# An earlier layernorm pipeline around the inverse FFT rounds, and a first MLP matmul loop in quarters instead of halves

## The chip, the cores and the metric

The kernel runs on one core of one Trainium2 chip. The metric is the device time of one execution, in microseconds. "Span" is the length of the one profiled execution; timed runs are longer by some 1.8 us. In the profile PE is TensorE, DVE is VectorE, ACT is ScalarE, POOL is GpSimd and SPq is the queue of SyncE, which here issues the DMA transfers. L512 is line 512 of the kernel file.

## The reference

A long convolution by FFT sits between two layernorms and is followed by two MLPs. Sequence length is 2048 and width 640, so there are 16 tiles of 128 positions. Cut to what matters:

```python
h = _layernorm(x) * (1 + ca) + sa
x = x + ga * conv_h3(h, A_k, A_v, ...)       # kv -> FFT -> product -> inverse FFT -> q * y
h = _layernorm(x) * (1 + cb) + sb            # "first" layernorm below, with its affine
# inside the MLP block, on h:
h1 = gelu(_layernorm(h) @ w1)                # "second" layernorm; w1 is 640 x 640
hs = shift_by_1_1_2_2(h1) @ w2               # four column groups shifted along the sequence
x1 = h + hs
out = x + gb * (x1 + gelu(_layernorm(x1) @ w3) @ w4)   # third layernorm; w3 is 640 x 1728
```

## The kernel before

The change lies in the stretch from the last inverse FFT step to the end of the first MLP loop. The inverse FFT delivers the 16 tiles in six rounds of three tiles (the last has one). For each tile VectorE forms y*q and adds the residual, ScalarE squares it, POOL turns the sums into mean and inverse deviation, VectorE does the affine of the first layernorm, ScalarE squares again, POOL finishes again, VectorE normalises into `hn`, and a DMA transpose writes it into `hnT`, on which the first MLP matmul works.

```python
def ln_finish(li, t0, t1):                    # eight tiny POOL instructions, 1 to 3 columns each
    n = t1 - t0
    bq, var, tmp = ...                        # [P, 4] F32
    nc.gpsimd.tensor_scalar(bq, s1, 1.0 / D, None, ALU.mult)
    nc.gpsimd.tensor_tensor(var, bq, bq, ALU.mult)
    nc.gpsimd.tensor_scalar(var, var, -1.0, EPS, ALU.mult, ALU.add)
    nc.gpsimd.tensor_scalar(tmp, s2, 1.0 / D, None, ALU.mult)
    nc.gpsimd.tensor_tensor(var, var, tmp, ALU.add)
    nc.gpsimd.tensor_tensor(rstds[:, li, t0:t1], var, mhalf, ALU.pow)
    nc.gpsimd.tensor_tensor(tmp, bq, rstds[:, li, t0:t1], ALU.mult)
    nc.gpsimd.tensor_scalar(nbs[:, li, t0:t1], tmp, -1.0, None, ALU.mult)

def consume(A, yps2):                         # y*q, residual, square
    t = work.tile([P, 4, 160], BF, name="yq", tag="yq")
    for h in range(2):
        nc.vector.tensor_tensor(t[:, 2*h:2*h+2, :], yps2[h], qv[:, 2*h:2*h+2, :], ALU.mult)
    nc.vector.scalar_tensor_tensor(x1_all[:, A, :], t, 1.0, x1_all[:, A, :], ..., accum_out=sums[:, 0, 0, A:A+1])
    nc.scalar.activation(junk, x1_all[:, A, :], ACT.Square, accum_out=sums[:, 0, 1, A:A+1])

def ln_stage_b(tiles):                        # affine of the first layernorm, square
    for t in tiles:
        nc.vector.tensor_scalar(u, x1_all[:, t, :], rstds[:, 0, t:t+1], nbs[:, 0, t:t+1], ALU.mult, ALU.add)
        nc.vector.tensor_tensor(u, u, cb1, ALU.mult)
        nc.vector.scalar_tensor_tensor(h_all[:, t, :], u, 1.0, sbv, ..., accum_out=sums[:, 1, 0, t:t+1])
        nc.scalar.activation(junk, h_all[:, t, :], ACT.Square, accum_out=sums[:, 1, 1, t:t+1])

def ln_stage_d(tiles):                        # normalise, transpose
    for t in tiles:
        hn = work.tile([P, D], BF, name="hn", tag="hn")           # two buffers
        nc.vector.tensor_scalar(hn, h_all[:, t, :], rstds[:, 1, t:t+1], nbs[:, 1, t:t+1], ALU.mult, ALU.add)
        nc.sync.dma_start_transpose(hnT[:, :, t*P:(t+1)*P], hn)

def pipeline_step(r):                         # called after round r
    if 0 <= r - 1 < NR: ln_finish(0, ...)     # of round r-1
    if 0 <= r - 2 < NR: ln_stage_b(rounds[r - 2])
    if 0 <= r - 3 < NR: ln_finish(1, ...)     # of round r-3
    if 0 <= r - 4 < NR: ln_stage_d(rounds[r - 4])

w3_sb, w4_sb = ...                            # in memory that the FFT and q have used; loads issued here

for hf in range(2):                           # first MLP loop: two halves of 1024 positions
    for fb in range(ND):                      # five blocks of 128 output columns
        ps2 = psB.tile([P, 2, 512], F32, name="ps_l1", tag="q2")
        for scl in range(2):
            for b in range(ND): nc.tensor.matmul(ps2[:, scl, :], w1 block, hnT[:, b, 512 positions])
        # GELU of the 1024 positions, shifted, cut where a column group or a partition rule asks for it
        for (p0, p1) in _legal_pieces(...):
            nc.scalar.activation(gsT[p0:p1, fb, ...], psf[p0:p1, ...], ACT.Gelu_apprx_tanh)
# ... second MLP loop (tile by tile: matmul, residual, square, ln_finish(2), normalise, transpose),
# ... third and fourth MLP loops, output
```

The order in which instructions stand in each engine's queue is chosen when the kernel is built, by a scheduler that works from the order of the source; what it chose can be read in the trace.

## Time and profile before

The kernel took 496.61 us, the median of 4 runs (495.66 to 497.45). The profiled execution has a span of 493.8 us.

| us from the span's start | before |
|---|---|
| first y*q on VectorE | 248.7 |
| first normalise (`hn`) | 285.7 |
| last square of the two layernorms ends on ScalarE | 301.9 |
| first GELU starts | 305.6 |
| last transpose lands | 317.6 |
| last GELU ends | 328.7 |
| second MLP loop starts on VectorE | 327.6 |
| third MLP loop starts on TensorE | 347.7 |

The first lines of the profile's page give the busy time of each engine; the next line gives the chain that ended last. No engine is busy for more than two thirds of the span: the kernel is a relay of stages, and each stage has to be read by itself.

```profile
span 493.8 us, 8042 instructions
...
PE 314.8 (64%) x3092; PEld 183.4 (37%) x3092; DVE 234.0 (47%) x565; ACT 224.2 (45%) x319; POOL 91.4 (19%) x227
...
PE 38%; DVE 23%; DMA 17%; ACT 10%; issue 5%; SPq 4%; POOL 2%; DVEq 0%; POOLq 0%; ACTq 0%
```

The chain of waits, in order of time, for the end of the stage (start, duration, what). A piece "DMA KSb<-hn" is a transpose, from its issue to its landing.

```profile
302.61 2.57 DMA KSb<-hn
305.27 0.46 DVE hn L519
...
314.57 0.46 DVE hn L519
315.05 2.58 DMA KSb<-hn
...
317.76 1.25 PE ps_l L568 x5
319.04 1.00 ACT B L579
```

The chain steps from a transpose (about 2.6 us) to the normalise that waited for its buffer (0.46 us) and on to the next transpose. There are two `hn` buffers, so the tiles come in pairs. The last transpose lands at 317.63, and the second half of the GELUs can only then begin.

ScalarE's own timeline (start, duration, line, instruction, output and input; in brackets how long it was idle before, and what ended that):

```profile
301.11 0.74 ACT L514 ACTIVATE junk<-KSb 128x640 bf16<-128x640 bf16 x1 [1.08 <-DVE B L558]
...
301.96 1.28 ACT L579 ACT_TABLE_LOAD   x1
305.59 3.09 ACT L579 ACTIVATE B<-ps_l 128x1024 bf16<-128x1024 f32 x3 [2.35 <-PE ps_l L568]
...
315.06 0.28 ACT L588 ACTIVATE B<-ps_l 128x31 bf16<-128x31 f32 x2
319.04 1.00 ACT L579 ACTIVATE B<-ps_l 128x992 bf16<-128x992 f32 x1 [3.69 <-PE ps_l L568]
...
326.61 2.06 ACT L579 ACTIVATE B<-ps_l 32x1024 bf16<-32x1024 f32 x2
```

In this trace ScalarE works through its queue in order. The last square of the layernorms (301.11) is followed by every GELU of the loop. The first GELU waited 2.35 us for TensorE: in this kernel a group of matmuls covers 1024 positions, so it needs eight transposed tiles. The tenth normalise started at 303.83 after a wait that ended on a transpose; with two buffers that is the eighth tile's, which therefore landed at about 303.8, just before the five last matmuls of that group. From 315.34 ScalarE idles 3.69 us, for the last eight tiles.

The queue of SyncE (start, time over which the issues are spread, what, count):

```profile
277.42 0.39 SPq L553 DMA_DIRECT2D B<-in_B_w_dram  x1
278.05 0.70 SPq L552 DMA_DIRECT2D B<-in_B_w_dram  x1
286.12 2.77 SPq L520 DMA_TRANSPOSE KSb<-hn  x2
...
293.24 23.01 SPq L520 DMA_TRANSPOSE KSb<-hn  x14
```

Two weight loads of 2080 and 2160 KB (w4 and w3) were issued just before the first transposes.

### The profile page before, as it was taken

How to read it: one execution, taken by the hardware profiler on the slowest of the kernel's cores; microseconds unless marked ns; L12 is line 12 of the kernel's file. 1: busy time of each engine (PE TensorE's matmuls, PEld its weight loads, DVE VectorE, ACT ScalarE, POOL GpSimd, SP SyncE). 2: the span in 40 equal slices, each digit the busy share in tenths (PEclk: the TensorE clock that was granted, in tenths of full speed). 3: DMA queues.
4: the chain of work that ended last, by engine and by line, in shares of the span. 5: the costliest groups of instructions: out<-in, count | busy, mean ns of one | idle time of the engine just before them, and what ended most of it. 6: DMA issues, size and time to landing. Idle time of an engine off the chain costs nothing.

```text
span 493.8 us, 8042 instructions
## 1 busy us (share of the span) xinstructions
PE 314.8 (64%) x3092; PEld 183.4 (37%) x3092; DVE 234.0 (47%) x565; ACT 224.2 (45%) x319; POOL 91.4 (19%) x227
## 2 busy tenths in 40 slices
PE   0115859759778200683043109799399999999994
PEld 0112433549557200673011003245134444445552
DVE  3049518204699765791089995137200000344443
ACT  2165552787667422383035445677945444000000
POOL 1045100000002222000038787024600000000000
PEclk9999998989999855698555557999879999999998
DMA  8991694340205532007900485303440000011111
GB/s 278 399 232 33 106 118 56 56 182 33 56 9 148 159 87 79 16 3 147 279 3 3 140 267 100 66 2 66 93 55 0 1 0 1 20 38 40 39 41 41
DMA packets 74463, 43.14 MB, mean 87 GB/s; under 512 B 56952, under 2 KB 72632, under 8 KB 74168
## 3 DMA queue, kind: packets, MB, share of 16 engines
q1 hardware_dynamic: 71592, 38.69, 32.6%
q10 hardware_dynamic: 2064, 2.62, 1.6%
q0 software_dynamic: 768, 1.31, 1.2%
q8 instruction: 24, 0.39, 0.3%
q14 instruction: 15, 0.12, 0.1%
HBM read 29.50 MB, written 7.86 MB: 76 GB/s over the span
## 4 chain that ended last, share of the span: by engine, by line
PE 38%; DVE 23%; DMA 17%; ACT 10%; issue 5%; SPq 4%; POOL 2%; DVEq 0%; POOLq 0%; ACTq 0%
PE ps_l L640 14%; PE ps_l L631 12%; DMA B<-in_A_v_dram 5%; DMA B<-q_scr 4%; PE ps_s L169 4%; ACT B L261 4%; DMA KSb<-hn 4%; DVE B L263 3%; DVE B L502 2%; DVE yq L493 2%; PE ps_l L599 2%; DVE KSb L512 2%; DMA xt<-in_A_q_dram 2%; DVE TA L183 2%; SPq L342 2%
## 5 line engine op out<-in xcount | busy, mean ns | idle before, releaser
L631 PE MATMUL ps_l<-KSb,B 128*128 128x512 bf16 (+1 forms) x280 | 63.9, 391 | 8.4 <-DMA KSb<-xn 8.4
L643 DVE TENSOR_TENSOR bo<-ps_l,KSb 128x512 bf16<-128x512 f32 x16 | 11.1, 691 | 109.4 <-PE ps_l L640 109.4
L261 ACT CAST B<-ps_s 128x1024 bf16<-128x1024 f32 (+1 forms) x46 | 38.9, 961 | 18.3 <-PE ps_s L157 13.3
L631 PEld LDWEIGHTS <-B 128*128 128x128 bf16 (+1 forms) x280 | 28.0, 101 | 43.9 <-issue 7.2
L192 PE MATMUL ps_s1i<-ESs,TA 64*128 64x128 bf16 x320 | 20.5, 230 | 37.0 <-DVE TA L183 37.0
L169 PE MATMUL ps_s<-B,Gs 64*64 64x320 bf16 x512 | 38.5, 305 | 7.0 <-DVE B L263 3.9
L209 PE MATMUL ps_out<-B,Hs 32*32 32x160 bf16 x512 | 13.5, 310 | 40.2 <-DVE yq L493 39.0
L169 PEld LDWEIGHTS <-Gs 64*64 64x64 bf16 x512 | 35.0, 110 | 10.5 <-issue 6.8
L568 PE MATMUL ps_l<-KSb,Gs 128*128 128x512 bf16 x100 | 25.0, 413 | 20.8 <-DMA KSb<-hn 19.9
L361 PE MATMUL ps_ksh<-kT,diagw 128*128 128x512 bf16 x80 | 21.8, 432 | 19.8 <-DVE diagw L326 16.2
L505 ACT ACTIVATE junk<-B 128x640 bf16<-128x640 bf16 x16 | 11.8, 737 | 37.4 <-DVE B L502 37.4
L438 POOL TENSOR_SCALAR ln_rstd<-ln_mv 128x1 f32<-128x1 f32 x16 | 4.1, 256 | 130.5 <-DVE ln_mv L435 130.5
L157 PE MATMUL ps_s<-F1bd,B 128*128 128x256 bf16 x160 | 21.5, 272 | 9.1 <-ACT B L261 5.5
L640 PE MATMUL ps_l<-B,B 128*128 128x512 bf16 (+1 forms) x160 | 27.3, 301 | 0.0
L192 PEld LDWEIGHTS <-TA 64*128 64x128 bf16 x320 | 13.5, 102 | 37.2 <-issue 37.2
L442 ACT ACTIVATE xh<-xt,ln_nb,ln_rstd 128x640 bf16<-128x640 bf16 x16 | 14.7, 920 | 26.8 <-DVE ln_nb L440 15.6
L493 DVE TENSOR_TENSOR yq<-ps_out,B 128x320 bf16<-128x320 f32 x32 | 14.2, 480 | 24.5 <-DMA B<-q_scr 24.5
L263 DVE CAST B<-ps_s 128x640 bf16<-128x640 f32 (+1 forms) x26 | 24.4, 965 | 0.0
L261 ACT CAST B<-ps_s1i 128x1024 bf16<-128x1024 f32 x20 | 19.3, 1017 | 10.8 <-PE ps_s1i L192 10.8
L568 PEld LDWEIGHTS <-Gs 128*128 128x128 bf16 x100 | 10.3, 105 | 35.4 <-DMA KSb<-hn 17.7
L209 PEld LDWEIGHTS <-Hs 32*32 32x32 bf16 x512 | 5.5, 100 | 48.0 <-issue 47.9
L640 PE MATMUL ps_l<-B,Gs 128*128 128x512 bf16 (+1 forms) x128 | 22.6, 299 | 0.0
(119 smaller groups left out, 648.5 us busy)
## 6 DMA issues: line engine op xcount, KB each, us to landing
KSb<-in_w_mod_dram SPq DMA_DIRECT2D x1, 4800.0 KB
B<-in_A_v_dram ACTq DMA_DIRECT2D x1, 2560.0 KB
B<-in_A_k_dram SPq DMA_DIRECT2D x1, 2560.0 KB
xt<-in_A_q_dram SPq DMA_DIRECT2D x64, 40.0 KB
B<-kv_scr SPq DMA_DIRECT2D x1, 2560.0 KB
q_scr<-qt SPq DMA_DIRECT2D x16, 160.0 KB
B<-in_A_q_dram SPq DMA_DIRECT2D x4, 640.0 KB
B<-q_scr SPq DMA_DIRECT2D x1, 2560.0 KB
```

The source lines that it names most:

```text
L157: nc.tensor.matmul(psv[:, ml, :], lhsT=xf[:, m * 128:(m + 1) * 128], rhs=rhs, start=True, stop=True)
L169: nc.tensor.matmul(ps[64 * g:64 * g + 64, kl, 0:320], lhsT=Gs[64 * g:64 * g + 64, k2, c, cp, :], rhs=T1[64 * g:64 * g + 64, c * 32 + k2, : ...
L192: nc.tensor.matmul(psv[:, g, ql, :], lhsT=T[64 * g:64 * g + 64, cp, 4 * lq:4 * lq + 4, :].rearrange("p a k -> p (a k)"), rhs=ESs[64 * g:64 ...
L209: nc.tensor.matmul(pss[j4 // 2][32 * cg:32 * cg + 32, j4 % 2, a * 160:(a + 1) * 160], lhsT=Hs[32 * j4:32 * j4 + 32, n1, cpp, :], rhs=ZS[32 ...
L261: nc.scalar.copy(dst, src)
L263: nc.vector.tensor_copy(dst, src)
L361: nc.tensor.matmul(ps[:, scl, :], lhsT=diagw[:, b, j, :], rhs=kT[:, 16 - j + sc * 512:16 - j + sc * 512 + 512], start=(j == 0), stop=(j == 3))
L442: nc.scalar.activation(xh[:], xt[:], ACT.Identity, scale=rstd[:], bias=nb[:])
L493: nc.vector.tensor_tensor(t[:, 2 * h:2 * h + 2, :], yps2[h], qv[:, 2 * h:2 * h + 2, :], ALU.mult)
L568: nc.tensor.matmul(ps2[:, scl, :], lhsT=w1_sb[:, b, fb * P:(fb + 1) * P], rhs=hnT[:, b, sc * SC:(sc + 1) * SC], start=(b == 0), stop=(b == ...
L631: nc.tensor.matmul(ps2[:fw, scl, :], lhsT=w3_sb[:, b, fb * P:fb * P + fw], rhs=xnT[:, b, sc * SC:(sc + 1) * SC], start=(b == 0), stop=(b = ...
L640: nc.tensor.matmul(ps2[:, bank, 0:n1 - n0], lhsT=g3_slices[fb][:fw, t * P:(t + 1) * P], rhs=w4_sb[:fw, fb, n0:n1], start=(fb == 0), stop=( ...
```

## The change

The intent: let the normalise and the transposes start earlier, by handling the second layernorm of a round one round sooner, and let the GELUs start and end closer to the transposes, by going through the first MLP loop in four quarters of 512 positions rather than in two halves of 1024. The arithmetic is the same. I call the two parts the pipeline half and the loop half.

```diff
-def inverse_stage2(nc, psum_pool, ZS, Hs, consume, after_round=None):
+def inverse_stage2(nc, psum_pool, ZS, Hs, consume, after_round=None, before_round=None):
     for r in range(6):
+        if before_round is not None:
+            before_round(r, tilesA)
 ...
-    def pipeline_step(r):
+    def pipeline_pre(r):
         if 0 <= r - 1 < NR:
             ln_finish(0, tl[0], tl[-1] + 1)
         if 0 <= r - 2 < NR:
-            ln_stage_b(rounds[r - 2])
-        if 0 <= r - 3 < NR:
-            tl = rounds[r - 3]
+            tl = rounds[r - 2]
             ln_finish(1, tl[0], tl[-1] + 1)
-        if 0 <= r - 4 < NR:
-            ln_stage_d(rounds[r - 4])
+
+    def pipeline_post(r):
+        if 0 <= r - 1 < NR:
+            ln_stage_b(rounds[r - 1])
+        if 0 <= r - 2 < NR:
+            ln_stage_d(rounds[r - 2])
 ...
-    for hf in range(2):
-        for fb in range(ND):
+    for sc in range(S // SC):
+        n1_lo, n1_hi = 16 * sc, 16 * sc + 16
+        for fbp in ((0, 1), (2, 3), (4,)):
             ps2 = psB.tile([P, 2, 512], F32, name="ps_l1", tag="q2")
-            for scl in range(2):
-                sc = 2 * hf + scl
+            for j, fb in enumerate(fbp):
                 for b in range(ND):
-                    nc.tensor.matmul(ps2[:, scl, :], ...)
+                    nc.tensor.matmul(ps2[:, j, :], ...)
 ...               # the GELU code runs once for each fb of fbp, on 512 positions
```

More of the change, by code (lines that the diff above doesn't have):

```diff
@@ L529, in pipeline_step, with before_round @@
         if 0 <= r - 2 < NR:
-            ln_stage_b(rounds[r - 2])
-        if 0 <= r - 3 < NR:
-            tl = rounds[r - 3]
+            tl = rounds[r - 2]
             ln_finish(1, tl[0], tl[-1] + 1)
-        if 0 <= r - 4 < NR:
-            ln_stage_d(rounds[r - 4])
-    def after_round(r, tiles):
-        rounds[r] = tiles
-        pipeline_step(r)
-    inverse_stage2(nc, psA, ZS, Hs, consume, after_round)
-    for r in range(NR, NR + 4):
-        pipeline_step(r)
+    def pipeline_post(r):
[3 more added lines that the diff above has]
+            ln_stage_d(rounds[r - 2])
+    def before_round(r, tiles):
+        rounds[r] = tiles
+        pipeline_pre(r)
+    def after_round(r, tiles):
+        pipeline_post(r)
+    inverse_stage2(nc, psA, ZS, Hs, consume, after_round, before_round)
+    for r in range(NR, NR + 2):
+        pipeline_pre(r)
+        pipeline_post(r)
     if dbg is not None and "x1" in dbg:
@@ L561 @@
     SC = 512
-    for hf in range(2):
-        for fb in range(ND):
+    for sc in range(S // SC):
+        n1_lo, n1_hi = 16 * sc, 16 * sc + 16
+        for fbp in ((0, 1), (2, 3), (4,)):
             ps2 = psB.tile([P, 2, 512], F32, name="ps_l1", tag="q2")
-            for scl in range(2):
-                sc = 2 * hf + scl
+            for j, fb in enumerate(fbp):
                 for b in range(ND):
-                    nc.tensor.matmul(ps2[:, scl, :], lhsT=w1_sb[:, b, fb * P:(fb + 1) * P], rhs=hnT[:, b, sc * SC:(sc + 1) * SC],
+                    nc.tensor.matmul(ps2[:, j, :], lhsT=w1_sb[:, b, fb * P:(fb + 1) * P], rhs=hnT[:, b, sc * SC:(sc + 1) * SC],
@@ L569 @@
                                      start=(b == 0), stop=(b == ND - 1))
-            psf = ps2[:].rearrange("p a b -> p (a b)")
-            n1_lo, n1_hi = 32 * hf, 32 * hf + 32
-            f0 = fb * P
-            while f0 < (fb + 1) * P:
-                gidx = f0 // CQ
-                f1 = min((fb + 1) * P, (gidx + 1) * CQ)
-                sh = shifts[gidx]
-                m_lo, m_hi = max(n1_lo, -sh if sh < 0 else 0), min(n1_hi, 64 - sh if sh > 0 else 64)
-                for (p0, p1) in _legal_pieces(f0 - fb * P, f1 - fb * P):
-                    nc.scalar.activation(gsT[p0:p1, fb, 32 * (m_lo + sh):32 * (m_hi + sh)],
-                                         psf[p0:p1, 32 * (m_lo - n1_lo):32 * (m_hi - n1_lo)], ACT.Gelu_apprx_tanh)
-                    for n1s in list(range(n1_lo, m_lo)) + list(range(m_hi, n1_hi)):
-                        n1d = n1s + sh
-                        o = 32 * (n1s - n1_lo)
-                        if n1d >= 64:
-                            nc.scalar.activation(gsT[p0:p1, fb, 32 * (n1d - 64) + 1:32 * (n1d - 64) + 32],
-                                                 psf[p0:p1, o:o + 31], ACT.Gelu_apprx_tanh)
-                        else:
-                            nc.scalar.activation(gsT[p0:p1, fb, 32 * (n1d + 64):32 * (n1d + 64) + 31],
-                                                 psf[p0:p1, o + 1:o + 32], ACT.Gelu_apprx_tanh)
-                f0 = f1
@@ new lines @@
+            for j, fb in enumerate(fbp):
+                psf = ps2[:, j, :]
+                f0 = fb * P
+                while f0 < (fb + 1) * P:
+                    gidx = f0 // CQ
+                    f1 = min((fb + 1) * P, (gidx + 1) * CQ)
+                    sh = shifts[gidx]
+                    m_lo, m_hi = max(n1_lo, -sh if sh < 0 else 0), min(n1_hi, 64 - sh if sh > 0 else 64)
+                    for (p0, p1) in _legal_pieces(f0 - fb * P, f1 - fb * P):
+                        nc.scalar.activation(gsT[p0:p1, fb, 32 * (m_lo + sh):32 * (m_hi + sh)],
+                                             psf[p0:p1, 32 * (m_lo - n1_lo):32 * (m_hi - n1_lo)], ACT.Gelu_apprx_tanh)
+                        for n1s in list(range(n1_lo, m_lo)) + list(range(m_hi, n1_hi)):
+                            n1d = n1s + sh
+                            o = 32 * (n1s - n1_lo)
+                            if n1d >= 64:
+                                nc.scalar.activation(gsT[p0:p1, fb, 32 * (n1d - 64) + 1:32 * (n1d - 64) + 32],
+                                                     psf[p0:p1, o:o + 31], ACT.Gelu_apprx_tanh)
+                            else:
+                                nc.scalar.activation(gsT[p0:p1, fb, 32 * (n1d + 64):32 * (n1d + 64) + 31],
+                                                     psf[p0:p1, o + 1:o + 32], ACT.Gelu_apprx_tanh)
+                    f0 = f1
```

## The prediction

> **What bounds the kernel now.** By the chain of waits the span (493.8 us) is a relay of stages; the last 135 us (third and fourth MLP matmuls, 26% of the chain) are not touched. The change lies in 248.7 to 328.7 us. Until 300.7 VectorE is the chain: the timeline shows no gap over 0.6 us, at 1.55 us a tile for y*q and residual, 1.51 for the second layernorm's affine, 0.36 for the normalise. POOL is nearly as full: one ln_finish (eight tiny instructions) takes 4.3 to 4.9 us, back to back. Then 16 DMA transposes end it, in pairs of about 3.1 us, because the normalised tile has two buffers; the last lands at 317.6. Then the second half of the GELUs: the second MLP matmul starts in earnest at 326.6, ScalarE's last GELU ends at 328.7.
>
> **What the change does.** No arithmetic is removed. (a) In the instruction order the first normalise comes after 6 affines and 9 tiles of y*q, not 9 and 15. (b) The GELUs become 36 of about 512 columns instead of 18 of about 1024. Measured: 1.015 us for 1024 columns, 0.1 to 0.19 for 31; so 512 is estimated at 0.57, and all GELUs at 22 us instead of 19.4. (c) Only a quarter of the GELUs is left after the last transpose: about 7 us instead of 11. (d) The two large weight loads now stand between transposes. Before, two transposes issued at 286.1 and 287.4, behind these loads, moved no small packets until about 291, when the large ones had passed. I expect the sixth and seventh transposes to wait likewise.
>
> **Sum along the new order, with measured durations.** The first affine waits 1.2 us for POOL. Normalises run from 273 instead of 286; eight transposes are issued by 296. But POOL's queue now has the second-layernorm finish of round 3 ahead of the first-layernorm finish of the last tile; at 4.6 us each, VectorE's affine of tile 15 waits 2.5 to 4 us, and eight normalises stand behind it. The last affine is done near 306 (300.7 before), the last transpose lands near 318 to 319. ScalarE issues in order: all GELUs stand behind the last square, so they start near 309 (305.6 before), then run nearly without the 3.7 us pause of before: 309 + 22 = 331, against 328.7. The same sum for the kernel before gives 302.0 for the last square (trace: 301.8) and 316.0 for the last transpose (317.6). So POOL's order and the GELU overhead give the early start back: net about +2.3 us.
>
> The Trainium skill ("SBUF — State Buffer", "SBUF: two separate sides") says VectorE and GpSimd exclude each other on a shared port; the trace agrees: ln_finish takes 4.6 us under busy VectorE, 2.6 when it idles.
>
> **Predicted: 498.9 us, 8 in 10 between 494.5 and 503. Faster by over 2%: 0.02; within 2%: 0.95; slower by over 2%: 0.03.**
>
> **Right if** the timeline shows: first normalise at 272 to 275; tile 15's affine waiting on POOL over 2 us; first GELU at 307 to 311, GELUs busy 21 to 22 us; the sixth transpose landing after the first weight load; the second MLP loop starting 1 to 4 us later than 326.6; later stages unchanged.
>
> **Wrong if** POOL is quick enough that tile 15 doesn't wait (then -1 us), if a GELU is cheaper than 0.57, or if TensorE, idle until GELUs free PSUM, runs the first MLP loop at half clock and becomes the limit (+3 us).

## The result, and the profile after

A ratio here is the mean time of one kernel's runs over the mean of the other's runs in the same rounds, so it is not quite the ratio of the medians that I quote. Executions over 1.5% slower than the fastest of the same kernel are left out of the means.

The changed kernel took 496.97 us (median of 11 runs, 495.43 to 499.49); the kernel before took 496.24 us in the same rounds (16 runs, 495.42 to 499.33). The ratio is 1.0018, with a 95% interval of 0.9998 to 1.0037.

The start of the stage, the first y*q, varied between 245.9 and 250.6 us among the profiles, although the instructions ahead of it hardly differ; the same kernel of two labels (`loop_only` and `loop_only_again` below) had 247.0 and 248.1. I therefore count from the first y*q of each profile and judge a kernel's stage by that:

| us after the first y*q, one profile each | before | after |
|---|---|---|
| first normalise | 36.9 | 23.3 |
| last square ends | 53.2 | 56.8 |
| last transpose issued | 66.3 | 66.4 |
| first GELU starts | 56.9 | 58.1 |
| last GELU ends | 79.9 | 79.8 |
| second MLP loop starts on VectorE | 78.9 | 79.6 |
| third MLP loop starts on TensorE | 99.0 | 99.5 |
| from there to the end of the span | 146.1 | 146.4 |

The page of the changed kernel, its first lines and its chain by engine:

```profile
span 493.6 us, 8062 instructions
...
PE 318.5 (65%) x3092; PEld 183.5 (37%) x3092; DVE 233.9 (47%) x565; ACT 226.0 (46%) x337; POOL 88.7 (18%) x227
...
PE 36%; DVE 21%; DMA 15%; ACT 15%; issue 5%; POOL 4%; SPq 2%; DVEq 0%; ACTq 0%; POOLq 0%
```

In the chain DMA has fallen from 17% to 15% and ACT has risen from 10% to 15%: the transposes no longer carry the end of the stage, the GELUs do. ScalarE's timeline after:

```profile
303.80 0.74 ACT L516 ACTIVATE junk<-KSb 128x640 bf16<-128x640 bf16 x1 [1.03 <-DVE B L566]
...
304.64 1.28 ACT L587 ACT_TABLE_LOAD   x1
305.94 1.64 ACT L587 ACTIVATE B<-ps_l 128x512 bf16<-128x512 f32 x3
...
311.53 10.96 ACT L587 ACTIVATE B<-ps_l 128x512 bf16<-128x512 f32 x19
...
326.38 1.21 ACT L587 ACTIVATE B<-ps_l 32x512 bf16<-32x512 f32 x2
```

No GELU waits any more: they run from 305.94 to 327.6. But they start right behind the last square and its table load, and that square is 3.6 us later than before, counted from the first y*q. VectorE's waits in the second half of the pipeline, two of them, say why:

```profile
293.86 0.45 DVE L521 TENSOR_SCALAR hn<-KSb,rstds,nbs 128x640 bf16<-128x640 bf16 x1 [1.60 <-DMA KSb<-hn]
...
300.66 0.45 DVE L512 TENSOR_SCALAR u_ln<-B,rstds,nbs 128x640 bf16<-128x640 bf16 x1 [1.05 <-POOL nbs L484]
```

The first is a normalise that waited 1.60 us for a buffer that a transpose still held; the second is the affine of the last tile, which waited 1.05 us for POOL. The third part of the delay is no wait: on VectorE ten normalises of 0.36 us now stand ahead of the end of the last affine, where seven stood before. The sum fits: from the first y*q to the last instruction of the last affine VectorE took 51.18 us before (299.91 - 248.73) and 55.05 us after (302.88 - 247.83), 3.9 us more, of which waits are 2.5 (2.65 against 0.15) and three more normalises 1.1; 0.3 us are left over. The queue of SyncE:

```profile
271.64 12.90 SPq L522 DMA_TRANSPOSE KSb<-hn  x5
284.64 0.52 SPq L561 DMA_DIRECT2D B<-in_B_w_dram  x1
285.26 3.16 SPq L522 DMA_TRANSPOSE KSb<-hn  x1
288.54 0.50 SPq L560 DMA_DIRECT2D B<-in_B_w_dram  x1
...
302.63 12.78 SPq L522 DMA_TRANSPOSE KSb<-hn  x8
```

The sixth transpose, at 285.26, stands behind a weight load. The eighth normalise, which needs that transpose's buffer, is the one that waits until 293.86: 8.5 us after the issue, where others took 2.6. The Trainium skill ("DMA: Bandwidth & Descriptors", "Queues, rings and completion order") says that each of the DMA engines takes the descriptors of one ring in order; this trace agrees, and so does that of before, where the transposes issued at 286.1, behind two loads, moved no small packets before 290 (a transpose's packets are small, under 512 B; the loads' are larger).

POOL, in the stretch where the affine of the last tile waits for it:

```profile
288.97 0.36 POOL L476 TENSOR_SCALAR lnf_b<-sums 128x3 f32<-128x3 f32 x1 [2.00 <-DVE B L504]
...
292.99 0.23 POOL L484 TENSOR_SCALAR nbs<-lnf_t 128x3 f32<-128x3 f32 x1
...
296.66 0.37 POOL L476 TENSOR_SCALAR lnf_b<-sums 128x1 f32<-128x1 f32 x1
...
300.40 0.22 POOL L484 TENSOR_SCALAR nbs<-lnf_t 128x1 f32<-128x1 f32 x1
```

One finish runs from 288.97 to 293.2 (4.25 us), the next to 296.7 (3.50 us), the next from 296.66 to 300.6 (3.96 us). VectorE stood still for 0.97, 0.66 and 1.01 us of them. Before 288.97 POOL had been idle for 2.0 us.

### The profile page after: what moved, and what is told of

The parts are those of the page before. It is cut to its first block, busy times and chain, and to the rows that moved or that the text cites. A ratio compares the mean times of both kernels' runs of the same rounds, so it can differ in the third digit from the quotient of the medians.

```text
span 493.6 us, 8062 instructions
## 1 busy us (share of the span) xinstructions
PE 318.5 (65%) x3092; PEld 183.5 (37%) x3092; DVE 233.9 (47%) x565; ACT 226.0 (46%) x337; POOL 88.7 (18%) x227
## 4 chain that ended last, share of the span: by engine, by line
PE 36%; DVE 21%; DMA 15%; ACT 15%; issue 5%; POOL 4%; SPq 2%; DVEq 0%; ACTq 0%; POOLq 0%
PE ps_l L648 14%; PE ps_l L639 11%; DMA B<-in_A_v_dram 5%; PE ps_s L169 4%; DMA B<-q_scr 4%; ACT B L263 4%; ACT B L587 4%; DVE B L265 3%; DMA KSb<-xn 2%; DVE B L504 2%; PE ps_ksh L363 2%; PE ps_l L607 2%; DVE yq L495 2%; DVE TA L183 2%; DMA xt<-in_A_q_dram 2%
## 5 line engine op out<-in xcount | busy, mean ns | idle before, releaser
L192 PE MATMUL ps_s1i<-ESs,TA 64*128 64x128 bf16 x320 | 19.7, 225 | 36.9 <-DVE TA L183 36.9
L363 PE MATMUL ps_ksh<-kT,diagw 128*128 128x512 bf16 x80 | 22.8, 447 | 20.1 <-DVE diagw L328 16.2
L576 PE MATMUL ps_l<-KSb,Gs 128*128 128x512 bf16 x100 | 27.5, 441 | 10.7 <-DMA KSb<-hn 5.6
L157 PE MATMUL ps_s<-F1bd,B 128*128 128x256 bf16 x160 | 23.0, 286 | 9.0 <-ACT B L263 5.3
L211 PEld LDWEIGHTS <-Hs 32*32 32x32 bf16 x512 | 5.5, 100 | 54.2 <-issue 54.1
L495 DVE TENSOR_TENSOR yq<-ps_out,B 128x320 bf16<-128x320 f32 x32 | 14.3, 481 | 23.6 <-DMA B<-q_scr 23.6
L607 PE MATMUL ps_l<-Gs,B 128*128 128x512 bf16 (+1 forms) x160 | 22.2, 299 | 1.2 <-ACT B L593 1.1
```

Of the source, the lines that this page charges most:

```text
L157: nc.tensor.matmul(psv[:, ml, :], lhsT=xf[:, m * 128:(m + 1) * 128], rhs=rhs, start=True, stop=True)
L192: nc.tensor.matmul(psv[:, g, ql, :], lhsT=T[64 * g:64 * g + 64, cp, 4 * lq:4 * lq + 4, :].rearrange("p a k -> p (a k)"), rhs=ESs[64 * g:64 ...
L363: nc.tensor.matmul(ps[:, scl, :], lhsT=diagw[:, b, j, :], rhs=kT[:, 16 - j + sc * 512:16 - j + sc * 512 + 512], start=(j == 0), stop=(j == 3))
L495: nc.vector.tensor_tensor(t[:, 2 * h:2 * h + 2, :], yps2[h], qv[:, 2 * h:2 * h + 2, :], ALU.mult)
L576: nc.tensor.matmul(ps2[:, j, :], lhsT=w1_sb[:, b, fb * P:(fb + 1) * P], rhs=hnT[:, b, sc * SC:(sc + 1) * SC], start=(b == 0), stop=(b == N ...
L607: nc.tensor.matmul(ps2[:, bank, 0:n1 - n0], lhsT=gsT[:, b, t * P:(t + 1) * P], rhs=w2_sb[:, b, n0:n1], start=(b == 0), stop=(b == ND - 1))
```

## The experiments

All kernels gave correct results. Times of one batch share the runs of the kernel before: 496.95 us (11 runs) for the first four, 496.64 us (11 runs) for the next four, 496.34 us (11 runs) for the last four. By the 2% rule of the record every one of these runs is "same"; the intervals below tell which differences are clear of the noise.

My theory: the end of the stage is set by ScalarE's queue, which holds the last square, then the table load, then every GELU. What moves the last square moves the end. Early transposes are worth nothing as such; the loop half is worth what it lets ScalarE begin earlier, less the cost of more GELU instructions. Rivals: the pipeline half does gain, by its early transposes; the loop half is worth nothing, since splitting the GELUs eats what it saves; or not ScalarE but TensorE or the transposes set the end of the GELUs, so that an earlier start of them is lost again in waits. Where an expectation calls a theory by a letter, B is the rival of the split GELUs and C that of a limit outside ScalarE.

Read together afterwards, the profiles confirm the theory for the changed kernel and its variants, but not for the kernel before and the two halves. Two paths lead to the last GELU, and the later one sets the end:

| us after the first y*q | ScalarE's waits for TensorE among the GELUs | first GELU | last transpose issued | last GELU ends | after the last transpose's issue | after the first GELU |
|---|---|---|---|---|---|---|
| before | 3.69 | 56.9 | 66.3 | 79.9 | 13.6 | 23.1 |
| pipe_only | 2.81 | 59.2 | 67.6 | 81.2 | 13.6 | 22.0 |
| loop_only | 0.99 | 54.5 | 66.6 | 77.3 | 10.7 | 22.8 |
| loop_table | 0.62 + 1.06 | 52.9 | 65.7 | 76.4 | 10.7 | 23.6 |
| after | none | 58.1 | 66.4 | 79.8 | 13.4 | 21.65 |
| after_early_table | none | 56.9 | 66.6 | 78.5 | 12.0 | 21.6 |
| loop_table_hn4 | none | 56.8 | 62.1 | 78.5 | 16.4 | 21.65 |

Where ScalarE pauses among the GELUs, the last one ends at a fixed distance from the last transpose: 13.6 us with halves, 10.7 us with quarters (loop_only_again, best_a and best_b have 10.7 too), wherever the first GELU starts. Where it doesn't pause, the last one ends about 21.65 us after the first GELU, wherever the last transpose is. So ScalarE's queue is the limit in the changed kernel, and the last transpose is the limit in the kernel before and in either half alone.

### pipe_only: the pipeline half alone

```diff
 # the changed kernel, with the first MLP loop of before
-    for sc in range(S // SC):
-        for fbp in ((0, 1), (2, 3), (4,)):
+    for hf in range(2):
+        for fb in range(ND):
```

> Only the layernorm half of the change; the first MLP loop stays as before. Instruction order on VectorE and the DMA queue is that of the changed kernel. Markers are counted from the first y*q on VectorE. Theory A (the early transposes buy nothing, because the pipeline half makes VectorE reach the last square 3.7 us later, and ScalarE takes GELUs only after its last square): last square ends near 56.8 us (53.1 before), last transpose lands near 69 as in both kernels, first GELU near 58, second MLP loop starts on VectorE near 79 (78.9 before, 79.6 changed): time ratio to before 0.999 to 1.002. Rival B (the pipeline half gains, the GELU splitting loses): ratio 0.994 to 0.997, second loop near 76.

Measured: 496.48 us (6 runs), ratio 1.0003 [0.997, 1.0035]. The first normalise came at 24.2 us after the first y*q (before 36.9), the last square ended at 57.9 (before 53.2), the first GELU started at 59.2 and the second loop at 80.2, so 1.25 us later than before. ScalarE no longer waited for the first GELU (2.35 us before) and its pause in the middle was 2.81 us (3.69 before), so the early transposes did take 3.2 us of waiting away. But the queue came to its first GELU 4.7 us later (59.2 against 56.9 - 2.35). Normalises that come 13 us earlier bought nothing; the first rival falls. The ratio met the expectation (the second loop came 1.2 us later than it says), but not for the reason that I gave there, for the end still waits for the last transposes. TensorE waits for one, and ScalarE for TensorE:

```profile
317.06 8.36 PE L576 MATMUL ps_l<-KSb,Gs 128*128 128x512 bf16 x38 [2.07 <-DMA KSb<-hn]
...
318.33 1.00 ACT L587 ACTIVATE B<-ps_l 128x992 bf16<-128x992 f32 x1 [2.81 <-PE ps_l L576]
```

The last eight transposes still come at the end of VectorE's pipeline, issued from 55.9 to 67.6 (before from 53.9 to 66.3): the last one 1.3 us later, and the last GELU ended 1.3 us later.

### loop_only: the loop half alone

```diff
 # the kernel before, with the first MLP loop of the change
-    for hf in range(2):
-        for fb in range(ND):
+    for sc in range(S // SC):
+        for fbp in ((0, 1), (2, 3), (4,)):
```

> Only the loop half of the change; VectorE, POOL and DMA queue in the order of before. Theory A: last square ends near 53.1 us after the first y*q, so the table load ends and the GELUs start near 54.4, 1.2 to 4 us earlier than in either kernel; they end near 76 (then the last transpose at 69 plus 7 us is the limit), the second loop starts on VectorE near 76: 2.9 us less than before, ratio 0.992 to 0.996. Rival B (GELU splitting costs 2.3 us of ScalarE and that is what ate the gain): second loop near 80 or later, ratio 1.000 to 1.004.

Measured: 491.97 us (6 runs), ratio 0.9915 [0.9888, 0.9942]. The last square ended at 53.2 as before, the first GELU started at 54.5 (before 56.9), the second loop at 77.1 (before 78.9), where I had expected 76; the ratio is just under the range that I expected. ScalarE's timeline:

```profile
299.41 0.74 ACT L514 ACTIVATE junk<-KSb 128x640 bf16<-128x640 bf16 x1 [1.08 <-DVE B L558]
...
300.26 1.28 ACT L579 ACT_TABLE_LOAD   x1
301.55 1.64 ACT L579 ACTIVATE B<-ps_l 128x512 bf16<-128x512 f32 x3
...
318.63 0.57 ACT L579 ACTIVATE B<-ps_l 128x480 bf16<-128x480 f32 x1 [0.99 <-PE ps_l L568]
```

Compare the third line with that of before: the first GELU follows the table load at once, since a group of matmuls needs four transposed tiles instead of eight. The pause of 3.69 us has shrunk to 0.99. Those two save 2.35 + 2.70 = 5.05 us of waiting, and the longer GELUs cost 2.27 us of it (21.65 us in the changed kernel, where they run without a pause, against 315.34 - 305.59 + 328.67 - 319.04 = 19.38 us before). The last GELU ends 2.6 us earlier than before. The rival of the split GELUs falls. By the table above the gain itself comes from the other side: with quarters less work is left after the last transpose (10.7 us instead of 13.6), and the earlier first GELU goes into the pause. The Trainium skill ("Perfetto Trace Analysis", "Optimizing Scalar/DVE Operations") says that where ScalarE or VectorE isn't saturated but causes bubbles on other engines, breaking up instructions may let work be completed sooner; this run agrees (the second loop, which waits for the GELUs, starts 1.8 us earlier), with the price of 2.27 us beside it.

### after_early_table: the change, with the GELU table loaded before the stage

```diff
     sums = statp.tile([P, 3, 2, NT], F32, name="sums")
+    warm = statp.tile([P, 1], BF, name="warm")
+    nc.scalar.activation(warm[:], ZS[:, 0, 159:160], ACT.Gelu_apprx_tanh)   # after the last evacuation
```

> The changed kernel with one extra one-column GELU right after the inverse transform's first stage, where ScalarE idles, so that the activation table load (1.28 us) no longer stands between the last square and the first GELU. Theory A (ScalarE's queue from last square to last GELU is the limit): first GELU 1.2 to 1.3 us earlier (near 56.9 after the first y*q), last GELU and second loop 1.2 us earlier, ratio to before 0.9975 to 1.000 where the changed kernel has 1.0018. Rival C (the last transpose, or TensorE at half clock, is the limit): first GELU earlier, but the second loop unmoved.

Measured: 493.61 us (6 runs), ratio 0.9955 [0.9925, 0.9985]. The last square stayed where it was (57.0), the first GELU came at 56.9, so 1.2 us earlier than in the changed kernel, and the last GELU and the second loop came 1.2 us earlier too (78.4 instead of 79.6). The ratio lies below the 0.9975 to 1.000 that I expected; see the end of this section. For the changed kernel the rival of a limit outside ScalarE falls: what ScalarE gains at the start of the GELUs arrives whole at their end. The timeline, last square and first GELUs:

```profile
306.81 0.74 ACT L518 ACTIVATE junk<-KSb 128x640 bf16<-128x640 bf16 x1 [1.03 <-DVE B L568]
...
307.54 1.62 ACT L589 ACTIVATE B<-ps_l 128x512 bf16<-128x512 f32 x3
```

### after_short01: the change, with a shorter finish for the first two layernorms

```diff
-    nc.gpsimd.tensor_scalar(bq, s1, 1.0 / D, None, ALU.mult)
+    nc.gpsimd.tensor_scalar(bq, s1, -1.0 / D, None, ALU.mult)
     nc.gpsimd.tensor_tensor(var, bq, bq, ALU.mult)
-    nc.gpsimd.tensor_scalar(var, var, -1.0, EPS, ALU.mult, ALU.add)
-    nc.gpsimd.tensor_scalar(tmp, s2, 1.0 / D, None, ALU.mult)
-    nc.gpsimd.tensor_tensor(var, var, tmp, ALU.add)
+    nc.gpsimd.tensor_scalar(tmp, s2, 1.0 / D, EPS, ALU.mult, ALU.add)
+    nc.gpsimd.tensor_tensor(var, tmp, var, ALU.subtract)
     nc.gpsimd.tensor_tensor(rstds[:, li, t0:t1], var, mhalf, ALU.pow)
-    nc.gpsimd.tensor_tensor(tmp, bq, rstds[:, li, t0:t1], ALU.mult)
-    nc.gpsimd.tensor_scalar(nbs[:, li, t0:t1], tmp, -1.0, None, ALU.mult)
+    nc.gpsimd.tensor_tensor(nbs[:, li, t0:t1], bq, rstds[:, li, t0:t1], ALU.mult)
```

> The changed kernel with the statistics finish of the two layernorms of this stage in six POOL instructions instead of eight (same result). It tests the step of the prediction that was too large: tile 15's affine waited 1.05 us for POOL, not 2.5 to 4. A finish should take 3.2 to 3.6 us instead of 4.1, the wait of tile 15 go to 0, the last square end 1.0 us earlier, first GELU near 57.1, second loop 1.0 us earlier; ratio about 0.998 to 1.001. If POOL's pace is shared with VectorE in a way that a shorter queue slows VectorE less or more, the gain differs; if POOL is no limit at all, nothing moves.

Measured: 494.9 us (6 runs), ratio 0.9966 [0.9938, 0.9995]. The wait of the last tile's affine for POOL is gone, the last square ended at 55.7 (56.8 in the changed kernel), the first GELU came at 57.0 and the second loop at 78.6. The ratio is again a little better than the range expected (0.998 to 1.001). So POOL was worth 1.1 us of the last square and not the 2.5 to 4 us of the prediction. (In this one profile the granted clock dipped to 0.71 early in the second MLP loop, so its later part is not to be compared.)

### after_early_w4: the change, with the fourth MLP weights loaded long before

The 13 full blocks of w4 get memory of their own and their load is issued about 100 us earlier; one buffer of the third MLP moves into the memory that they leave. (With w3 and w4 both in memory of their own the kernel didn't build, for want of room. Moving both loads behind the loop in the source left SyncE's queue unchanged, since the scheduler moved them back.)

```diff
+    w4_sb = wtp.tile([P, NF - 1, D], BF, name="w4t")
+    nc.sync.dma_start(w4_sb[:], B_w4[0:(NF - 1) * P, :]...)
 ...
-    w4_sb = B3[:, 10240:10240 + NF * D]...
-    nc.sync.dma_start(w4_sb[:, 0:NF - 1, :], ...)
+    w4_tail = B3[:, 16384:16384 + D]
 ...
-    g3x = g3p.tile([P, 3, S], BF, name="g3x")
+    g3x = B3[:, 10240:10240 + 3 * S]...
```

> The changed kernel with the first of the two large weight loads (13 of 14 blocks of w4) taken out from between the transposes: it has its own buffer and is loaded some 100 us earlier. In the changed kernel tile 7's normalise waits 1.6 us for the transpose of tile 5, which stands behind that load; here that wait should be gone. But POOL then has 1.6 us less for its queue, so tile 15's affine should wait longer for POOL than 1.05 us: the last square ends 0.3 to 1.0 us earlier than in the changed kernel (56.8 after the first y*q), not 1.6. Ratio to before 0.999 to 1.002. If the two waits were independent, the last square would end at 55.2.

Measured: 493.75 us (4 runs), ratio 0.9941 [0.9907, 0.9975]. The wait for the transpose's buffer was gone. The affine of the last tile waited 1.04 us for POOL, not longer than in the changed kernel as I had expected. The last square ended at 56.1, within what I expected, but the first GELU started at 53.1 and the second loop at 77.0, which is better than I expected. The reason is in ScalarE's timeline:

```profile
297.65 1.28 ACT L589 ACT_TABLE_LOAD   x1
298.94 0.60 ACT L589 ACTIVATE B<-ps_l 128x512 bf16<-128x512 f32 x1
299.44 0.73 ACT L519 ACTIVATE junk<-KSb 128x640 bf16<-128x640 bf16 x1
...
301.14 0.74 ACT L519 ACTIVATE junk<-KSb 128x640 bf16<-128x640 bf16 x1 [0.89 <-DVE KSb L517]
...
301.88 1.62 ACT L589 ACTIVATE B<-ps_l 128x512 bf16<-128x512 f32 x3
```

The table load and one GELU now stand ahead of the last two squares. The scheduler made another order of the same instructions, so the squares no longer hold the table load up. The size of the gain is thus not that of the weights alone. The profile does separate the parts: the last square is 0.7 us earlier, and a table load of 1.28 us and one GELU of 0.6 us no longer stand behind it; that is 2.6 us, and the second loop starts 2.6 us earlier than in the changed kernel. How much of the new order comes from the weights, the run doesn't tell. It agrees with the theory in what it shows of the queue: the GELUs start when the queue lets them.

### after_w4_short: after_early_w4 with the short finish as well

> The same with the short POOL finish of two runs ago as well: both waits gone, the last square ends near 54.1 to 54.5 us after the first y*q (56.8 changed, 55.7 with the short finish alone), first GELU near 55.6, second loop on VectorE near 77.3: the loss of the pipeline half is then these two waits (2.7 of 3.5 us). If the last square stays above 55.3, most of the loss lies in the order of VectorE's own work.

Measured: 492.34 us (4 runs), ratio 0.9906 [0.9886, 0.9926]. The last square ended at 55.3, later than the 54.1 to 54.5 that I expected, so by my own mark it stays open how much of the loss lies in the order of VectorE's work; a normalise still waited 0.60 us for a buffer, since w3's load still stands between the transposes. The first GELU started at 53.3, again ahead of the last two squares, and the second loop at 76.4 (77.3 expected).

### loop_table: the loop half alone, with the early table

> The loop half alone plus the early table load. In the loop half alone ScalarE waited 1.0 us for the first matmuls after the last transpose, so the last transpose is the limit there: with the table load gone the first GELU starts 1.25 us earlier (53.3 after the first y*q), but the second loop should not move (77.1, at most 0.2 earlier); ratio to before as in the loop half alone, 0.990 to 0.994. If ScalarE's queue were still the limit, the second loop would be 1.25 us earlier.

Measured: 492.56 us (5 runs), ratio 0.9918 [0.9903, 0.9933], the ratio of loop_only within the error. The second loop started at 76.2, so 0.9 us earlier than in loop_only, where I expected 0.2 at most. In this profile the last transpose was issued 0.9 us earlier too (65.7 against 66.6), and the last GELU ended 10.7 us after that issue in both, so it is the transposes that brought the gain: the GELUs started 1.7 us earlier and lost the rest in two waits for TensorE (0.62 and 1.06 us). Why the transposes came earlier isn't shown; best_b, the other kernel of this order with the early table, has 65.7 too.

### loop_table_hn4: four buffers for the normalised tile

```diff
-        hn = work.tile([P, D], BF, name="hn", tag="hn")
+        hn = work.tile([P, D], BF, name="hn", tag="hnb", bufs=4)
```

> The same with four buffers for the normalised tile instead of two, so transposes follow each other at the issue rate (1.3 us) and not in pairs of 3.1 us. The last transpose should be issued 2 to 3 us earlier (near 64 after the first y*q), ScalarE's GELUs then run without a pause from 53.3 to near 75, the second loop starts on VectorE near 75.3 to 76, ratio to before 0.987 to 0.991. If the second loop doesn't move against the loop half with the early table, the transposes were not the limit.

Measured: 495.25 us (6 runs), ratio 0.9981 [0.9949, 1.0014]. The last transpose was issued at 62.1 (65.7 in loop_table), so the transposes were indeed faster. But the kernel lost against loop_table: with free buffers the scheduler moved normalises forward in VectorE's queue, where they waited for POOL. One, at 299.61, stood ahead of the rest of the last affine, and the last square came later. Another, at 303.28, stood ahead of four small memsets that clear columns of the GELUs' output, and the first GELU waited 1.40 us for these (VectorE's lines, then ScalarE's):

```profile
299.61 0.45 DVE L521 TENSOR_SCALAR hn<-KSb,rstds,nbs 128x640 bf16<-128x640 bf16 x1 [1.38 <-POOL nbs L484]
...
303.28 0.45 DVE L521 TENSOR_SCALAR hn<-KSb,rstds,nbs 128x640 bf16<-128x640 bf16 x1 [1.37 <-POOL nbs L484]
303.69 0.13 DVE L560 MEMSET B<- 128x5 bf16 x4
...
303.87 1.64 ACT L581 ACTIVATE B<-ps_l 128x512 bf16<-128x512 f32 x3 [1.40 <-DVE B L560]
```

The last square ended at 55.4 (53.0 in loop_table), the first GELU started at 56.8 (52.9) and the second loop at 78.3 (76.2). My expectation failed. Transposes that are issued 3.6 us earlier, with a first GELU that starts 3.9 us later, cost 2.0 us: ScalarE's queue has become the limit. Of the 3.9 us, 2.4 are the square and 1.4 the memsets, so it isn't the last square alone that holds the GELUs.

### loop_only_again: the same kernel in another batch

> The same kernel as loop_only, timed again beside the combined versions. If the gain of the loop half is real and not a property of one set of rounds, the ratio to the kernel before lies between 0.987 and 0.996, and the second MLP loop starts on VectorE 76.5 to 78 us after the first y*q (before: 78.9). A ratio above 0.998 would mean that the loop half gains nothing dependable.

Measured: 493.77 us (6 runs), ratio 0.9944 [0.9921, 0.9967]; second loop at 77.0. The gain of the loop half is real; by the two batches it is 0.6 to 0.9%.

### best_a, best_b, best_c: combinations

All three have the early table and the short finish, the latter in all three layernorms. best_a is the loop half alone with early w4; best_b is the same with the weights where they were; best_c is the whole change (pipeline half too) with early w4.

> Loop half alone, plus the GELU table loaded early, plus the finish in six operations in all three layernorms, plus the fourth MLP weights loaded early. Theory (ScalarE's queue from last square to last GELU is the limit, then the second loop): second loop on VectorE 75.5 to 76.5 us after the first y*q, the second loop 0.5 to 1.5 us shorter than 20.0 us because ScalarE waits less for POOL there; ratio 0.984 to 0.991. Rival (POOL's finish is hidden in the second loop as well): second loop unchanged at 20.0 us, ratio as loop_table, 0.9915.

> Loop half alone, plus early table, plus the short finish in all three layernorms, weights where they were. Second loop on VectorE about 76.2 us after the first y*q, as in loop_table; second loop 0.5 to 1.5 us shorter than 20.0 us if POOL limits it, unchanged if not. Ratio 0.986 to 0.992. If best_a and best_b agree within 0.2%, the early weights are worth nothing where the late order of the normalises is kept.

> The whole change plus the early table, the short finish in all three layernorms and the early fourth weights. First GELU at 52 to 54 us and second loop at 75.4 to 76.5 us after the first y*q, ratio 0.985 to 0.991: with its delays of ScalarE's queue taken away, the pipeline half no longer costs anything. If it comes out over 0.5% slower than best_a, the pipeline half still costs by a way not named so far; if over 0.5% faster, the early transposes are of use after all once the queue is free.

| | time, us | ratio | last square ends | first GELU | second loop on VectorE | third loop on TensorE | from there to the end |
|---|---|---|---|---|---|---|---|
| best_a | 490.33 (5 runs) | 0.9881 [0.985, 0.9912] | 53.7 | 51.9 | 75.2 | 95.0 | 144.8 |
| best_b | 491.17 (6 runs) | 0.99 [0.9866, 0.9933] | 53.0 | 52.9 | 76.3 | 96.2 | 144.9 |
| best_c | 491.64 (6 runs) | 0.9907 [0.9878, 0.9936] | 57.0 | 53.3 | 77.1 | 97.0 | 144.7 |

best_a is faster than both kernels: the interval of its ratio to the kernel before ends at 0.9912, and the changed kernel's begins at 0.9998. The ratios of the three overlap, so the times do not order them.

The short finish did not shorten the second MLP loop as I had expected: from its start on VectorE to the first matmul of the third loop there are 19.9 us in best_a and best_b, as in loop_only (20.1 before). The gain came one step later. In the nine other profiles of this section and the two of the prediction the time from the third loop's first matmul to the end is 145.7 to 146.4 us, in these three 144.7 to 144.9. TensorE's timeline at the start of the third loop in loop_only, with the finish of eight instructions:

```profile
344.01 1.24 PE L631 MATMUL ps_l<-KSb,B 128*128 128x512 bf16 x5
347.61 1.24 PE L631 MATMUL ps_l<-KSb,B 128*128 128x512 bf16 x5 [2.36 <-DMA KSb<-xn]
```

and in best_b, with the finish of six:

```profile
343.18 1.24 PE L631 MATMUL ps_l<-KSb,B 128*128 128x512 bf16 x5
345.72 1.24 PE L631 MATMUL ps_l<-KSb,B 128*128 128x512 bf16 x5 [1.30 <-DMA KSb<-xn]
```

The second group of matmuls comes 3.60 us after the first in one and 2.54 us in the other: it waits for a transpose, and the tile to be transposed needs a finish of POOL. So the rival, that POOL is hidden inside the second loop, holds for the loop, and about 1.1 us of POOL's time lies open behind it.

best_c missed its expectation for the second loop (75.4 to 76.5 expected, 77.1 measured); best_a came 0.3 us earlier than expected. The last square of best_c is 3.3 us later than in best_a and its GELUs started 1.4 us later, the first after a wait of 1.27 us for TensorE; then ScalarE had one pause of 0.35 us. Even with the table, two of POOL's instructions and w4 taken out of the way, the pipeline half is not of use; whether it costs something is what its profile says (2.0 us at the second loop) and the times leave open (0.3%, within the error). Why TensorE was late there I have not settled. The ten matmuls ahead of that GELU ran from 49.3 to 53.3 us after the first y*q; in after_w4_short they ran from 49.3 to 52.9, and there the table load stood in the same wait. And w3's load was still in the way: a transpose behind it, issued at 285.94, took 8.8 us.

One thing stays open in the sizes. Counting what the stage and the rest gained in the profiles gives 0.7 us for after_early_table, 2.1 us for loop_only, 5.2 us for best_a, 4.0 for best_b, 3.4 for best_c; the times gained about 2.2, 4.2, 5.9, 5.0 and 4.6 us. The timed gains are larger by 0.7 to 2.1 us. One profile of a kernel can't tell whether the profile of before was a quick one (its timed run, 495.66 us, was the quickest of its four) or whether the time ahead of the stage differs between builds. So a timed gain of 1 or 2 us is not by itself evidence for a step of this argument; the places in the profiles are.

## Why the prediction was right or wrong, point by point

The class was right ("within 2%"), and 496.97 us lies in the range. The signed size was not: +2.3 us was predicted, and the runs show +0.9 us by the ratio (0.18% of 496), with an interval that includes zero; the profiles show +0.7 us at the start of the second loop. "The second MLP loop starting 1 to 4 us later" failed for the same reason.

The step of the prediction that failed is the size of one term: "POOL's queue now has the second-layernorm finish of round 3 ahead of the first-layernorm finish of the last tile; at 4.6 us each, VectorE's affine of tile 15 waits 2.5 to 4 us". The order of the queue was right, and the tile did wait for POOL. It waited 1.05 us. The three finishes that lead to it took 4.25, 3.50 and 3.96 us, 11.65 us from the first to the last instruction, where 4.6 us each would make 13.8; with these 2.15 us more the wait would have been 3.2 us (an estimate from the figures just given), inside the predicted range. I had taken 4.6 us for a constant, and had not even read the range rightly: in the profile before, ten finishes beside a VectorE that hardly paused took 3.9 to 4.9 us, not 4.3 to 4.9. Why these three were short isn't shown. VectorE paused in each of them, but a finish at 253.28, beside a VectorE that did not pause, took only 3.40 us. POOL was also not full: it had idled 2.0 us just before. And VectorE came to that affine 1.60 us late itself, because of the buffer wait that I had not foreseen; POOL worked on in that time. after_short01, which removes the wait for POOL, moved the last square by 1.1 us and no more. The buffer wait of 1.60 us is the opposite error, and it partly hid the first. The 1.2 us that I had given the first affine did not come at all. Together the last affine ended 55.9 us after the first y*q where I had put it at 57.3 (306 - 248.7), and from there to the first GELU it was 2.2 us where I had put 3. With the GELU start at 58.1 us after the first y*q instead of the predicted 60.3 (309 - 248.7), 2.2 of the 2.5 us between the predicted and the measured end of the GELUs are explained; 0.35 us is the GELU sum (22 predicted, 21.65 measured).

The other points:

- **The last square delayed, GELUs behind it: right.** The last square was 3.6 us later, and all GELUs stood behind it; the first, at 58.1, would be 306.8 on the clock of before, just ahead of the 307 to 311 that I had allowed. after_early_table shows this queue to be the limit of the changed kernel. That the kernel before was limited by its last transpose, as the prediction says, the profile confirms.
- **GELUs of 512 columns at 0.57 us, 22 us in all: right.** The common ones took 0.57 to 0.60 us, the whole 21.65 us. By the Trainium skill ("ScalarE: Activation LUTs", "What ACT_TABLE_LOAD costs") an activation has 186 ns beside its columns, of which about 93 overlap with the next; from that page I would estimate 18 more instructions at 18 x 93 ns = 1.7 us. The trace has 2.27 us.
- **The first affine waiting 1.2 us for POOL: wrong.** VectorE showed no such wait.
- **The sixth transpose held up by the weight load: right.** Its buffer came free 8.5 us after the issue. What I missed is that a normalise would wait 1.60 us for it, with the affines behind.
- **VectorE and GpSimd hindering each other: right in direction.** The Trainium skill's exclusive lock ("SBUF — State Buffer", "SBUF: two separate sides") fits finishes of 2.65 us with VectorE mostly idle against 3.9 to 4.9 us with VectorE busy in this stage of the kernel before. No experiment isolates it.
- **Later stages unchanged: right** (146.4 against 146.1 us).
- **TensorE at half clock as the limit: did not come about.** The granted clock was 0.50 from 300 to 304 us, and ten matmuls from 301.62 took 3.91 us, but they were done before the GELUs could start.

What the prediction also did not say, and should have, is that its own sum held a winning half. The loop half alone gives 0.6 to 0.9%; the pipeline half gives nothing and delays the square that the loop half's GELUs stand behind. The change is the sum of a gain and a loss of nearly the same size: at the second loop, -1.8 us alone and +1.25 us alone, and +0.7 together. The sum of the parts would be -0.5. The parts don't add because they meet different limits. Alone, the loop half leaves less work after the last transpose (10.7 us instead of 13.6), which is what limits there. With the pipeline half in, the last transpose comes at 66.4 us, so that path would end at 77.1 (66.4 + 10.7), but ScalarE's queue ends at 79.8 (58.1 + 21.65): the later start of the GELUs, which cost the pipeline half alone nothing while ScalarE still had a pause of 2.81 us, now counts in full.

## What to carry to other kernels

Where one stage hands over to the next, write down every path to the end of the new stage, with its last event and the work behind it: here the last transpose plus the GELUs that need it, and the first GELU plus all GELUs. Only the later path counts, and a change can move the limit from one to the other. For an engine that works through its queue in order, look for the last thing of the old stage that stands ahead of the first thing of the new one; feeding the new stage earlier from another side is worth nothing while that instruction is late. Take a change apart into its halves before accepting or rejecting it, since a good half can be hidden by a bad one. And don't carry one duration from one profile over to another kernel where it varies within the profile: size the wait with the short and the long value, and let the range of the prediction show both.

## What the Trainium skill lacked or had wrong

- "ScalarE: Activation LUTs", "What ACT_TABLE_LOAD costs": it gives about 1283 ns for the load and 1380 ns of drain, 2.66 us for a switch. The load took 1.28 us here, as stated, but the first GELU started directly behind it (304.64 + 1.28 = 305.92, GELU at 305.94), and loading the table early gained 1.2 us, not 2.7. The load itself began 0.01 us after the square's end. No drain of 1.4 us is seen.
- The same page and section: its fixed cost gives 1.7 us for 18 more activations, as estimated above; the trace has 2.27 us, 126 ns for each.
- "SBUF — State Buffer", "SBUF: two separate sides": it names the exclusive lock but no size for short GpSimd instructions beside a busy VectorE. Here a finish of eight instructions on 1 to 3 columns took from 2.65 us (VectorE mostly idle) to 4.9 us (VectorE busy).
- "DMA: Bandwidth & Descriptors", "Queues, rings and completion order": it has the order within a ring, but not what a transpose behind a large load pays: about 8.5 us instead of 2.6 us for a 128x640 tile behind 2.1 MB here.
- I found no page that says that the build-time order of instructions can outweigh the edit itself: early w4 weights let the first GELU pass the last two squares (53.1 against 58.1 us after the first y*q), and two more buffers let normalises pass the affines (last square 55.4 against 53.0).
